# Two empty turns between the first one-hot blocks and their products in an attention and routing kernel

## The chip, the cores and the metric

The kernel runs on one core of one Trainium2 chip. The metric is the device time in microseconds (us) of one execution. The engines are TensorE (PE: matrix products and transposes into PSUM), VectorE (DVE), ScalarE (ACT), GpSimd (POOL) and SyncE (SP, which issues most of the DMA transfers). Each engine works through its own queue in order; semaphores tie the queues together.

## The reference

```python
q_pool = q.reshape(B, H, S // 2, 2, D).mean(axis=3)          # B 4, H 8, S 1152, D 64
scores = softmax(q_pool @ k.T / sqrt(D)) ; attn = scores @ v  # 4 x 8 x 576 x 64
x = attn -> [2304 tokens, 512]
do_compute = x @ w_skip > 0                                   # tokens that go to an expert
e_idx = argmax(x @ w_gate) ; gate_w = its softmax probability # 8 experts
y = gate_w * relu(x @ w1[e_idx]) @ w2[e_idx] ; x = x + y      # for the tokens that compute
out = ((x @ m1) * (x @ m2)) @ w3 @ w_out                      # second block, all tokens
```

## The kernel before, in words

The 4 images of the batch have 8 heads each; two heads make a pair, so there are 16 pairs p, four to an image. A pair is worked in 9 tiles of 128 pooled queries. The loop (L772) runs over turns i; p and l are the quotient and remainder of i by 9. A turn is a software pipeline over tiles. In the order in which TensorE gets its work, turn i does this:

- 9 transposes (L305) of the softmax numerators of tile i - 2. ACT, VectorE and ACT evacuate the three banks (L324). After the second evacuation the loop calls `side("D")`, which gives one step to other work, described below.
- ACT's exponential of tile i - 1 (L294).
- 8 products with v (L341), which accumulate in one of two fixed banks, VB[0] or VB[1].
- 6 score products of tile i (L271; 9 with three operand pairs in the fifth tile of a pair), and VectorE's row maximum (L282).
- In turns with l in 8, 0, 1, 3, 4, 5, if a routing step of kind "P" is due, that step with the accumulation bank that is free (L828).
- Preparation of the pairs to come: POOL splits keys and queries into a high and a low part (`prep`, L224 to L238), and SP copies them to the operand tiles.

Two generators run beside this. `conv_ops` converts the weights of the last block from 64-bit numbers to 32-bit ones, in 40 chunks: POOL squares (L96), VectorE takes bits apart (L111 to L119), SP loads and stores. `route_ops(b)` routes image b: it begins at i = 44, 80 and 116 for images 0 to 2, and after the loop for image 3. It yields "P" ahead of a step for TensorE and "D" ahead of a small step for VectorE. `side(kinds)` advances the routing if the step due is of one of these kinds; otherwise the conversion.

Routing an image takes these steps: normalisers and gate products (two "P" steps), transposes of the logits (two), argmax and one-hot of the expert (five "D"), prefix sums (one "P", L408), index arithmetic (two "D"; the second ends with the cast into `hf_`, L434). Then POOL builds one-hot blocks, one for each 128 tokens, five in all, in a ring of two buffers `ob` (L441 and L444, four instructions each): two at once, each further one after the product of the block whose buffer it takes. A block's product on TensorE (two instructions, L465) writes token numbers to their slots, which VectorE adds to `slots` (L467). After the fifth come the gate sums (one "D", L479) and five "P" steps that transpose the attention output to rows (L487), scale them on VectorE (L490, L493) and store them (L495).

In image 3 the routing has a hook: VectorE builds all five blocks at once, and the products are at L456. After the loop follow the product of the two last weight matrices, the expert tiles and the last block.

Of the kernel before, what the change touches and what calls it, by code (L numbers as in the profile page):

```python
# [17 lines left out]
NE, D, F = 8, 512, 1024  # L18
# [26 lines left out]
def body(ctx, tc, q, k, v, w9, w1, w2, m1, m2, w3t, wo, cst, mcst, ids, out, dbg=None):  # L45
# [89 lines left out]
    if True:  # L135
# [13 lines left out]
        def tbank():  # L149
            return free["b"]  # L150
# [4 lines left out]
        def load(p):  # L155
            if p >= NP:
                return
            b, hp = divmod(p, NHP)
            rawq[p] = erl.tile([128, 2, SQ], F32, tag="qr", name="qr", bufs=2)
            rawk[p] = erl.tile([128, S], F32, tag="kr", name="kr", bufs=1)  # L160
            SP.dma_start(rawk[p], k[b, hp])
            SP.dma_start(rawq[p], q[b, hp])
# [23 lines left out]
        def load_v(p):  # L186
            if p >= NP:
                return
            b, hp = divmod(p, NHP)
            vr = mid.tile([128, 2, KT, HD], F32, tag="vr", name="vr", bufs=2)  # L190
            SP.dma_start(vr, v[b, 2 * hp:2 * hp + 2].rearrange("h (p t) d -> p h t d", p=128))
            rawv[p] = vr
# [21 lines left out]
        def ld_kh(h):  # L214
            SP.dma_start(f(KH[0][64 * h:64 * h + 64]), f(KS[0][h][0:64]))
# [137 lines left out]
        def route_ops(b, hook=None, obs=None):  # L353
# [84 lines left out]
            def build(j):  # L438
                t = ob[j] = obs[j % len(obs)]
                for u in range(2):  # L440
                    E.tensor_scalar(t[:, 128 * u:128 * u + 128], iota[:, 0:128], hf_[:, 0, u, j:j + 1], None,  # L441
                                    op0=ALU.is_equal)
                for u, c0, n in ((0, 256, NSL), (1, 256 + NSL, NCNT)):
                    E.tensor_scalar(t[:, c0:c0 + n], iota[:, 0:n], hf_[:, 1, u, j:j + 1], idf[:, b, j:j + 1],  # L444
                                    op0=ALU.is_equal, op1=ALU.mult)

            parts = ((0, 0, NSL), (1, NSL, NCNT))
            for j in range(len(obs)):
                build(j)
            if len(obs) == NTT:  # L450
                yield "P"
                tp = tbank()
                for u, c0, n in parts:
                    for j in range(NTT):
                        t = ob[j]
                        PE.matmul(tp[:, c0:c0 + n], lhsT=t[:, 128 * u:128 * u + 128], rhs=t[:, 256 + c0:256 + c0 + n],  # L456
                                  start=(j == 0), stop=(j == NTT - 1))
                DVE.tensor_tensor(slots, tp[:, 0:NSL + NCNT], slots, op=ALU.add)
            else:
                for j in range(NTT):  # L460
                    yield "P"
                    tp = tbank()
                    t = ob.pop(j)
                    for u, c0, n in parts:
                        PE.matmul(tp[:, c0:c0 + n], lhsT=t[:, 128 * u:128 * u + 128], rhs=t[:, 256 + c0:256 + c0 + n],  # L465
                                  start=True, stop=True)
                    DVE.tensor_tensor(slots, tp[:, 0:NSL + NCNT], slots, op=ALU.add)  # L467
                    if j + len(obs) < NTT:
                        build(j + len(obs))
# [30 lines left out]
        def side(kinds):  # L500
            k = rts.get("k")
            if k and k in kinds:
                rts["k"] = next(rts["g"], None)
            elif k != "D":
                next(conv, None)

        def emit_meta(scratch):
# [56 lines left out]
        def wprime_fill():  # L564
            wp = tctx.enter_context(tc.tile_pool(name="wp", bufs=1, side="right", reuse_waits="tile"))
            CC = [wp.tile([128, 8, D], F32R, name=f"CC{x}") for x in "hl"]
            RW = [wp.tile([128, 8, 128], F32, name=f"RW{i}") for i in range(3)]
            WS = [[wp.tile([128, 8, 128], F32R, name=f"WS{x}{i}") for x in "hl"] for i in range(3)]
            wv.update(CC=CC, RW=RW, WS=WS)
            wov = wd["wo"].rearrange("(a p f) -> p a f", p=128, f=D)  # L570

            def ld_rw(u):
                SP.dma_start(RW[u % 3], wd["w3t"].rearrange("(u p a f) -> u p a f", u=8, p=128, f=128)[u])
            wv["ld"] = ld_rw
            for u in range(2):
                ld_rw(u)
                SP.dma_start(f(CC[1][:, 4 * u:4 * u + 4]), wov[:, 4 * u:4 * u + 4])
            ld_rw(2)
            yield
            for u in range(3):  # L580
                POOL.tensor_scalar(WS[u][0], RW[u], 1.0, 0.0, op0=ALU.mult, op1=ALU.add)
                POOL.tensor_tensor(WS[u][1], RW[u], f(WS[u][0]), op=ALU.subtract)
                ld_rw(u + 3)
                yield
            for a in range(8):
                POOL.tensor_scalar(CC[0][:, a], f(CC[1][:, a]), 1.0, 0.0, op0=ALU.mult, op1=ALU.add)
                POOL.tensor_tensor(CC[1][:, a], f(CC[1][:, a]), f(CC[0][:, a]), op=ALU.subtract)
                if a % 2:
                    yield
# [158 lines left out]
        with tc.manual_schedule():  # L748
# [23 lines left out]
            for i in range(NSTEP + 7):  # L772
                p, l = divmod(i, NT9)
                if i == NSTEP - NT9 + 1:
                    for _ in conv:
                        pass
                    ectx.close()
                    wfill = wprime_fill()
                if i > NSTEP - NT9:
                    next(wfill, None)  # L780
                if l == (4 if p == 0 else 1):
                    load(p + 2)
                if l == 7 and p >= 1:
                    load_v(p + 1)
                it = i - 2
                tr = 0 <= it < NSTEP
                ss = i < NSTEP
                pvs = []
                for n in (2 * i - 13, 2 * i - 12):
                    pp, r = divmod(n, 18)  # L790
                    pvs.append((pp, *divmod(r, 9)) if 0 <= pp < NP else None)
                if (i - 36 - 8) >= 0 and (i - 36 - 8) % 36 == 0 and (i - 44) // 36 < NB - 1:
                    rts["g"] = route_ops((i - 44) // 36)
                    rts["k"] = next(rts["g"])
                if tr or ss:
                    st_s[i] = ps_s.tile([128, 3, 512], F32, tag="s", name="s")
                evac = []
                if tr:
                    for g in range(3):
                        emit_t(it, g, i, evac)  # L800
                        emit_c(it, g, EV[g], evac)
                        if g == 1 and i > 5:
                            side("D")
                if 1 <= i <= NSTEP:
                    emit_e(i - 1)
                for u in pvs:
                    if u:
                        emit_pv(*u)
                if ss:
                    for g in range(3):  # L810
                        emit_s(i, g, evac)
                    emit_x(i)
                    if i == 0:
                        prep_q(1, DVE, 0, 256, sq[1])
                        for c in range(3):
                            prep_k(1, 384 * c, 384 * c + 384)
                        ld_kh(1)
                        for h in range(2):
                            prep_q(h, POOL, 256, SQ, sr[h])
                        next(conv)  # L820
                        DVE.tensor_copy(base, cs[:, C_EOFF:C_EOFF + NC_])
                        DVE.tensor_copy(csr, cs[:, C_U:C_U + 256])
                    if i == 2:
                        PE.matmul(VB[1][:, 0:128], lhsT=ones, rhs=tri, start=True, stop=True)
                        DVE.tensor_copy(iota[:, 0:128], VB[1][:, 0:128])
                        DVE.tensor_scalar(iota[:, 128:NSL], iota[:, 0:NSL - 128], 128.0, None, op0=ALU.add)
                        DVE.tensor_scalar(idf, idt, 1.0, None, op0=ALU.add)
                if l in (8, 0, 1, 3, 4, 5) and rts.get("k") == "P":  # L828
                    free["b"] = VB[1] if l in (8, 0, 1) else VB[0]
                    side("P")  # L830
                if ss and p == 0 and l < 3:
                    prep(1, l)
                if i == 4:
                    next(conv)
                if ss and l >= 6:
                    prep(p + 2, l - 6)
                if ss and l in ((3, 4) if p == 0 else (4, 5)):
                    prep(p + 1, l if p == 0 else l - 1)
# [207 lines left out]
```

## Time and profile before

| | us |
|---|---|
| median of 3 runs | 1090.47 (1088.94 to 1090.56) |
| the profiled execution | 1092.66 |
| its span, first to last instruction | 1090.8 |
| TensorE busy in the span | 1038.4 (95%) |
| VectorE, ACT, POOL busy | 598.0, 482.4, 387.0 |
| the attention loop | about the first 558 us |

Rows of the timeline give the start, the duration, the engine, the line, the operation with output and inputs, and in brackets how long the engine had been idle before it and what released it. One row can merge neighbouring instructions of one line (x9); its duration is then from the first's start to the last's end. Ends of products are modelled and overlap the next product's start, so the pace of TensorE is read from start to start. A granted clock of 1.00 is 2.4 GHz, 0.50 is 1.2 GHz.

### The profile page before, as it was taken

The numbers are of one execution on the slowest core, as the hardware profiler recorded it, in microseconds if no ns is written. First come the engines' busy times: TensorE is split into PE (matmuls) and PEld (weight loads), VectorE is DVE, ScalarE is ACT, GpSimd is POOL, SyncE is SP. The second block draws the span as 40 slices with busy tenths as digits, with TensorE's granted clock in tenths as the row PEclk, the third lists the DMA queues.
The fourth block names the chain that finished last, engine by engine and source line by source line (L and its number), as shares of the span: only waits on it lengthen the run. The fifth ranks groups of instructions, "written<-read, shape, count | busy, mean of one in ns | idle before, by whom it ended". The sixth has DMA issues, their size and how long they took to land. (4 is left out here: it accounts for less than half of the span.)

```text
span 1090.8 us, 16927 instructions
## 1 busy us (share of the span) xinstructions
PE 1038.4 (95%) x6101; PEld 839.9 (77%) x6101; DVE 598.0 (55%) x934; ACT 482.4 (44%) x902; POOL 387.0 (35%) x426
## 2 busy tenths in 40 slices
PE   6999999999999999999999999998799999999996
PEld 5677776677766777667667778786799998989895
DVE  5888887688986888755637422437531221212120
ACT  4666666565665666555532322334432221212121
POOL 4754433672536724351620523439201010101101
PEclk9999999999999999989998999999899999999999
DMA  9887778377973678714702761507101010101000
GB/s 256 259 239 192 216 218 232 101 182 212 268 224 98 185 214 256 183 40 101 238 20 74 247 225 40 190 25 243 34 11 50 10 49 20 39 20 39 29 2 30
DMA packets 68237, 144.83 MB, mean 133 GB/s; under 512 B 12960, under 2 KB 22560, under 8 KB 68130
## 3 DMA queue, kind: packets, MB, share of 16 engines
q1 hardware_dynamic: 63330, 129.28, 41.1%
q0 software_dynamic: 4800, 14.24, 4.0%
q8 instruction: 53, 0.87, 0.3%
q14 instruction: 54, 0.44, 0.1%
HBM read 86.21 MB, written 22.87 MB: 100 GB/s over the span
## 5 line engine op out<-in xcount | busy, mean ns | idle before, releaser
L282 DVE TENSOR_REDUCE sm<-s 128x1 f32<-128x1152 f32 x144 | 195.2, 1356 | 108.4 <-PE s L271 88.3
L324 ACT COPY pt<-s 128x384 f32<-128x384 f32 x288 | 138.0, 479 | 184.4 <-PE s L305 184.1
L271 PE MATMUL s<-k,q 128*128 128x384 f32 x864 | 204.3, 364 | 15.5 <-DVE k L197 7.8
L271 PEld LDWEIGHTS s<-k,q 128*128 128x128 f32 x864 | 147.2, 193 | 83.8 <-issue 41.7
L294 ACT ACTIVATE p<-s,sm 128x1152 f32<-128x1152 f32 x144 | 176.3, 1225 | 10.0 <-DVE sm L282 9.7
L341 PE MATMUL vb<-pt,vr 128*64 128x256 f32 (+1 forms) x1152 | 173.9, 422 | 4.5 <-DVE xr L490 2.1
L305 PE MATMUL s<-cs,p 128*128 128x128 f32 x1296 | 172.0, 279 | 2.9 <-ACT p L294 2.9
L305 PEld LDWEIGHTS s<-cs,p 128*128 128x128 f32 x1296 | 151.5, 144 | 12.1 <-ACT p L294 6.2
L956 DVE TENSOR_TENSOR ar<-b,ar 128x384 f32<-128x384 f32 x48 | 26.8, 558 | 191.9 <-PE b L952 191.9
L341 PEld LDWEIGHTS vb<-pt,vr 128*64 128x64 f32 x1152 | 70.7, 137 | 59.4 <-issue 23.7
L971 POOL DMA_INDIRECT out_dram<-ar,slots x18 | 18.1, 1003 | 272.1 <-ACT ar L970 267.4
L324 DVE COPY pt<-s 128x384 f32<-128x384 f32 x144 | 78.9, 548 | 5.1 <-PE s L305 5.0
L225 POOL TENSOR_TENSOR kl<-kr,kh 128x384 fp32r<-128x384 f32 x45 | 47.6, 1058 | 73.0 <-DMA k<-kl 70.2
L957 ACT CAST CVh<-ar 128x384 fp32r<-128x384 f32 x48 | 24.6, 513 | 108.8 <-DVE ar L956 108.8
L96 POOL TENSOR_TENSOR cm<-ch 128x512 f32<-128x512 f32 x40 | 43.0, 1079 | 66.6 <-DVE ca L119 46.1
L560 PE MATMUL b<-W1h,CVh 128*128 128x512 f32 x176 | 60.5, 403 | 1.2 <-ACT CVh L691 0.7
L560 PE MATMUL b<-W2h,CVh 128*128 128x512 f32 x176 | 60.7, 405 | 0.3
L560 PE MATMUL b<-WPh,CVh 128*128 128x512 f32 x144 | 57.3, 398 | 0.0
L560 PE MATMUL b<-WPh,CVl 128*128 128x512 f32 x144 | 56.9, 395 | 0.0
L560 PE MATMUL b<-WPl,CVh 128*128 128x512 f32 x144 | 56.8, 395 | 0.0
L970 ACT COPY ar<-b 128x512 f32<-128x512 f32 x18 | 10.6, 586 | 86.2 <-PE b L560 86.2
L224 POOL TENSOR_SCALAR kh<-kr 128x384 fp32r<-128x384 f32 x45 | 27.2, 604 | 57.2 <-PE s L271 53.6
(210 smaller groups left out, 1816.7 us busy)
## 6 DMA issues: line engine op xcount, KB each, us to landing
R<-in_w_dram SPq DMA_DIRECT2D x16, 1024.0 KB, 7.1
vr<-in_v_dram SPq DMA_DIRECT2D x16, 576.0 KB
kr<-in_k_dram SPq DMA_DIRECT2D x15, 576.0 KB, 6.2
qr<-in_q_dram SPq DMA_DIRECT2D x15, 576.0 KB, 6.6
k<-kh SPq DMA_DIRECT2D x30, 288.0 KB, 5.6
k<-kl SPq DMA_DIRECT2D x30, 288.0 KB, 6.4
q<-qnl SPq DMA_DIRECT2D x60, 144.0 KB, 3.4
ch<-in_w3t_dram SPq DMA_DIRECT2D x16, 512.0 KB, 5.6
```

The costliest lines, as they stand in the source:

```text
L96: POOL.tensor_tensor(m, hf, hf, op=ALU.mult)
L224: POOL.tensor_scalar(KH[i][:, cc], rawk[p][:, cc], 1.0, 0.0, op0=ALU.mult, op1=ALU.add)
L225: POOL.tensor_tensor(KL[:, cc], rawk[p][:, cc], f(KH[i][:, cc]), op=ALU.subtract)
L271: m = PE.matmul(sp[:, c, 0:384], lhsT=lt, rhs=kk[:, 384 * c:384 * c + 384], start=(n == 0), stop=(n == len(seq) - 1))
L282: DVE.tensor_reduce(sm, sp[:, :, 0:384], axis=AX.XY, op=ALU.max, negate=True)
L294: ACT.activation(pt, sp[:, :, 0:384], AF.Exp, bias=sm, scale=1.0, accum_out=SM[b][:, hp, c:c + 1])
L305: m = PE.transpose(tp[:, u * 128:u * 128 + 128], src[:, kt * 128:kt * 128 + 128], ident)
L324: m = (DVE.tensor_copy(o, i_) if eng is DVE else ACT.copy(o, i_)).ins
L341: PE.matmul(acc[64 * h:64 * h + 64, 0:n], lhsT=vr[:, h, kt, :], rhs=pt[:, kt, h, :], start=(kt == 0), stop=(kt == KT - 1))
L560: PE.matmul(o, lhsT=lh[a], rhs=rh[b_], start=(first and n == 0), stop=(last and n == len(order) - 1))
L956: DVE.tensor_tensor(cv, pb[:, 0:GT], av, op=ALU.mult)
L957: ACT.copy(CV[0][:, c], cv)
```

## The change

After POOL has been given the first two blocks, the routing yields "C" twice, except for the image with a hook. The loop's call becomes `side("DC")`, so that a "C" step is passed there, one a turn. In such a turn the conversion advances as well, as it does in a turn in which no "D" step is due.

```diff
             for j in range(len(obs)):
                 build(j)
+            if not hook:
+                yield "C"
+                yield "C"
             if len(obs) == NTT:
                 yield "P"
...
             if k and k in kinds:
                 rts["k"] = next(rts["g"], None)
-            elif k != "D":
+            if kinds != "P" and k != "D":
                 next(conv, None)
...
                         if g == 1 and i > 5:
-                            side("D")
+                            side("DC")
```

## Rows read from the trace of the kernel before

**Rows 1.** The page: granted clock in 40 slices (tenths), and the costliest group.

```profile
PEclk9999999999999999989998999999899999999999
...
L282 DVE TENSOR_REDUCE sm<-s 128x1 f32<-128x1152 f32 x144 | 195.2, 1356 | 108.4 <-PE s L271 88.3
```

**Rows 2.** Waits of TensorE, whole span: total us, times, longest us.

```profile
PE s L271 <- DVE pt L324: 7.5, 11, 1.2
PE vb L465 <- POOL ob L444: 5.9, 3, 2.0
```

**Rows 3.** Timeline of TensorE, image 0, turns 55 to 59.

```profile
207.96 1.34 PE L271 MATMUL s<-k,q 128*128 128x384 f32 x6
211.29 0.75 PE L465 MATMUL vb<-ob 128*128 128x146 f32 x2 [1.99 <-POOL ob L444]
211.90 2.18 PE L305 MATMUL s<-cs,p 128*128 128x128 f32 x9
...
215.60 1.34 PE L271 MATMUL s<-k,q 128*128 128x384 f32 x6
216.78 1.14 PE L305 MATMUL s<-cs,p 128*128 128x128 f32 x9
...
220.04 0.28 PE L465 MATMUL vb<-ob 128*128 128x146 f32 x2
220.18 1.20 PE L305 MATMUL s<-cs,p 128*128 128x128 f32 x9
...
227.44 0.28 PE L465 MATMUL vb<-ob 128*128 128x146 f32 x2
```

**Rows 4.** Timeline of TensorE, image 1, turns 91 to 93.

```profile
344.54 1.34 PE L271 MATMUL s<-k,q 128*128 128x384 f32 x6
...
353.31 1.15 PE L305 MATMUL s<-cs,p 128*128 128x128 f32 x9
...
356.56 0.28 PE L465 MATMUL vb<-ob 128*128 128x146 f32 x2
```

**Rows 5.** Timeline of TensorE, image 2, turns 127 to 129.

```profile
481.65 1.34 PE L271 MATMUL s<-k,q 128*128 128x384 f32 x6
484.96 0.80 PE L465 MATMUL vb<-ob 128*128 128x146 f32 x2 [1.97 <-POOL ob L444]
...
491.71 1.15 PE L305 MATMUL s<-cs,p 128*128 128x128 f32 x9
```

**Rows 6.** Windows: length, busy us (instructions) by engine, granted clock, DMA share, GB/s.

```profile
211.80:215.20 3.40, 3.40 (x16) 2.65 (x18) 1.50 (x3) 1.56 (x3) 3.40 (x6) 0.50 0.00 0
215.30:348.00 132.70, 128.02 (x883) 95.69 (x879) 109.50 (x162) 82.22 (x157) 62.47 (x74) 1.00 0.72 200
...
484.90:491.60 6.70, 6.64 (x25) 5.04 (x26) 1.48 (x3) 2.17 (x4) 5.77 (x10) 0.50 0.37 93
```

**Rows 7.** Timeline of POOL, image 0, turns 55 to 62.

```profile
209.17 1.21 POOL L441 TENSOR_SCALAR ob<-iota,hf 128x128 fp32r<-128x128 f32 x2 [7.51 <-DVE hf L434]
...
214.06 1.63 POOL L441 TENSOR_SCALAR ob<-iota,hf 128x128 fp32r<-128x128 f32 x2
...
216.93 1.04 POOL L96 TENSOR_TENSOR cm<-ch 128x512 f32<-128x512 f32 x1
...
241.58 0.54 POOL L238 TENSOR_SCALAR bd<-qnl 64x64 fp32r<-64x64 f32 x2
```

**Rows 8.** Timeline of VectorE, turns 68, 71 and 138.

```profile
262.89 0.67 DVE L490 TENSOR_TENSOR xr<-vb,r 64x512 f32<-64x512 f32 x1
263.49 0.15 DVE L493 COPY xr<-ga 64x4 f32<-64x4 f32 x1
...
272.70 1.36 DVE L282 TENSOR_REDUCE sm<-s 128x1 f32<-128x1152 f32 x1
...
530.46 1.41 DVE L493 COPY xr<-ga 128x4 f32<-128x4 f32 x1
```

**Rows 9.** Waits of POOL, 0 to 560 us.

```profile
POOL kh L224 <- PE s L271: 53.6, 8, 17.3
```

## The prediction

> **What bounds the kernel now.** I read the page first. VectorE idles most before its maximum (L282), 108.4 us, of which score products of TensorE end 88.3 [rows 1]; so in the attention loop TensorE sets the pace, and idle time on it is time lost. Its granted clock is 9 tenths or more in every slice of the loop but the one from 464 us, which has an 8 [rows 1]: a first hint, and a coarse one, since a slice is 27 us long and hides a stretch of three. The list of TensorE's waits by line comes next [rows 2]. One group there has a single cause: the products of the one-hot blocks (L465) wait 5.9 us in three waits, 2.0 us at most, for POOL's L444.
>
> Then I opened TensorE's timeline around each of the three [rows 3 to 5]. In image 0, POOL starts the four one-hot instructions of block 0 at 209.17 us and is through block 1 at 214.06 [rows 7]; TensorE has finished its score products at about 209.3 and has block 0's product next in its queue. It starts that at 211.29 after 1.99 us of idling. What follows runs slowly: nine transposes take 2.18 us, where nine of the next turn take 1.14 [rows 3]. The windows say why: the granted clock is 0.50 (1.2 GHz) from 211.8 to 215.2, and 1.00 (2.4 GHz) from 215.3 to 348.0, up to the next of the three waits; the third is followed by 6.7 us at half clock [rows 6]. So each wait is paid twice: as idle time, and as slow work afterwards.
>
> **The change, step by step.** Number the turns of the loop by i; l is i mod 9. Image 0's routing starts at i = 44. At i = 55 (l = 1) its last index arithmetic runs and POOL gets blocks 0 and 1; in the same turn the product slot (l is in the list 8, 0, 1, 3, 4, 5) takes product 0. Now two "C" steps come between: i = 56 and 57 pass them, and the slot at the end of i = 57 (l = 3) takes product 0; products 1 and 2 go to 58 and 59, 3 and 4 to 62 and 63 (before: 55, 57, 58, 59, 62). The gate sums move from 63 to 64, the five blocks of transposed rows from 63, 64, 66, 67, 68 to 64, 66, 67, 68, 71. The weight conversion still advances in "C" turns, so it skips turn 64 instead of 63 and is otherwise unmoved. The same holds 36 and 72 turns later. The fourth image, after the loop, passes a hook and gets no empty turns. No instruction is added or removed.
>
> *What goes.* Image 0: from the start of the score products before the late product (207.96) to the transposes two turns on (216.78) are 8.82 us. Undisturbed, the same work is one set of score products, 215.60 to 216.78 = 1.18, and a turn without product, 216.78 to 220.04 = 3.26 [rows 3]. The product itself is still paid, later: 220.04 to 220.18 = 0.14, and 0.06 on the transposes behind it (1.20 against 1.14), together 0.20. Saved: 8.82 - 1.18 - 3.26 - 0.20 = 4.18. Image 1: 344.54 to 353.31 = 8.77; less 1.18, less 353.31 to 356.56 = 3.25, less 0.20: 4.14 [rows 4]. Image 2: 481.65 to 491.71 = 10.06; less 1.18, 3.25 and 0.20: 5.43 [rows 5]. Sum 13.8 us. Of image 0's 4.18, the part up to the transposes at 211.90 is 3.94 - 1.38 = 2.56 (waiting, with the second half of the product also late); 1.62 is slow clock.
>
> *What is late next.* Without the stall turn 56 ends at about 209.1 + 3.3 = 212.4 and turn 57 at 215.7. POOL is through block 1 at 214.06 as before, since its start hangs on VectorE's casts in turn 55; products 0 and 1 find their operands. Block 2 reuses block 0's buffer and starts after product 0, behind one square of the conversion (L96, 1.04 us [rows 7]) that the empty turns put ahead of it and that fits into POOL's idle time between 214.1 and 215.9. It needs 216.93 - 214.06 = 2.87 us at most and so is done by 219; product 2 comes two turns after product 0, 220.04 to 227.44 being 7.4 us [rows 3], at about 223. Cover: over 4 us. Block 3 has three turns, block 4 four.
>
> *What the moved pieces may cost.* Block 4 and the key and query splits behind it on POOL slide by up to 3 us against TensorE. Image 0's splits end at 242.12 [rows 7], and their copies to the operand tiles are issued in turn 67, near 256: 14 us of cover, cost nothing. Those copies go by SP's queue, in which the stores of transposed rows stand ahead of them as before. The last transposed block goes to turn 71 (l = 8), where POOL splits queries and VectorE has no idle time: its maximum at 272.70 begins without having waited for the score products [rows 8]. There 0.67 + 0.15 us are added (the 64-row forms of L490 and L493). How VectorE takes that no row shows; the nearest are a small copy of the same line that took 1.41 us instead of 0.15 while POOL worked [rows 8], and the longest wait of score products for VectorE's copy, 1.2 us [rows 2]. Ends: 0 and 1.2 per image; I take 0.4, nearer to the turns 66 to 68, which carry the same load and mostly show no wait, and for image 2 nothing, since turn 143 is the last with score products and the tail waits for ACT anyway. Together 0.8, ends 0 to 2.4. A gain there I exclude: work is only made later.
>
> The Trainium skill's page "SBUF — State Buffer", section "Who interferes with whom", says that VectorE and POOL share a pair of ports and that the second of two contending instructions waits for the whole of the first. The 1.41 us copy agrees [rows 8]. If every such copy in the moved blocks were held so, 1.26 us for each of two images, the sum would be 13.8 - 2.5 = 11.3.
>
> Net: 13.8 - 0.8 = 13.0. The profiled execution took 1092.66 us (span 1090.8 and 1.9 around it); with the change it would take 1079.7. The median of the timed runs is 1090.47, 2.2 less; the same 13.0 gives **1077.5 us**. Whether the timed runs have the long slow stretch of image 2 in the same place isn't shown: three images like image 0 would give 12.5, three like image 2 16.3, so 11.7 to 15.5 net of 0.8.
>
> **Rivals.**
> *A, the clock falls anyway.* If the half clock after 211.8 belonged to that place (its load, another engine) and not to the wait, only the waiting would be saved: 3 x 2.56 = 7.7, and 1082.8 us. For it: nothing but that the cause is inferred. Against: the slow stretches start within 0.6 us of a late product [rows 3, 5, 6], and the 132.7 us up to the next one are at full clock with the same work [rows 6]. The Trainium skill's page "TensorE: Matmul & The Clock Gate", section "HAM oscillation — how this bites in real kernels", warns of idle gaps longer than these, which speaks for A; the trace shows the fall after gaps of 2 us. Chance 0.07.
>
> *B, the wait moves to product 2.* If the square ahead of block 2 on POOL waited (for its load, or for a buffer), block 2 would be late and TensorE would idle at turn 59. It begins to cost from 4 us of delay and has taken the gain when the delay is 6.5 us (2.5 of waiting, then the slow clock). Only images 0 and 1 still convert; image 2's 5.4 stay: about 1085 us. Against: in the shown stretch the square ran without idling before it [rows 7]. Chance 0.05.
>
> *C, slower.* POOL's builds now end one product later, and the key and query splits of the pair after next queue behind them. If these reached the operand tiles late, the first score products of that pair would wait, and the slow clock would follow: 1.62 us and the wait. It decides from 14 us of delay on POOL, and loses more than the gain from about 17 (three more of waiting); at 18 us, 1 us per image is lost, 1093 us. Against: POOL idles 53.6 us before L224 waiting for TensorE's score products [rows 9], so it is ahead, not behind. Chance 0.03.
>
> *D, nothing moves.* If the two steps were swallowed (the slot rule would let product 0 in at turn 56 if l = 2 were in its list, which it isn't), 1090.5. Chance 0.02.
>
> **How the numbers follow.** Forecast 0.83, A 0.07, B 0.05, C 0.03, D 0.02. The forecast's own range is 1074.5 (gain 15.5 with a little beside it) to 1080 (11.3, less the spread of the runs, which cover 1.6 us). Stretched to A's edge: 1074.0 to 1082.0, which leaves out B to D, most of A and some of the forecast's own ends. 0.2% is 2.2 us, about what a measurement of this kernel tells from no change: faster by more than that, 0.94 (forecast, A, most of B); within it 0.03 (D, the rest of B); slower 0.03 (C).
>
> **What would show it.** In the profile after: no wait of L465 for POOL's L444 in the list of waits; product 0 some 6.5 us after POOL's first one-hot instruction, without idle before it; the granted clock 1.00 throughout from 30 us to the end of the loop; the three stretches 4.2, 4.1 and 5.4 us shorter; at turns 71 and 107 a wait of score products for L324 of some tenths. The forecast is wrong if a slow stretch stays where no wait precedes it (A), if L465 waits again at its third product (B), or if L271 waits for the splits of the keys (C).

## The result, and the profile after

The changed kernel takes 1076.76 us (median of 4 runs, 1076.03 to 1080.15) against 1089.93 us before: 13.2 us less, ratio 0.9886 with a 95% interval of 0.9863 to 0.9909. In two later comparisons the ratio was 0.9909 (0.9885 to 0.9933) and 0.9916 (0.9890 to 0.9942); by the medians of the three, 13.2, 11.9 and 9.0 us are gained. The profiled execution has a span of 1074.2 us against 1090.8.

TensorE's longest waits after, whole span (total us, times, longest us). The one-hot products are L468 now, three lines lower, and stand nowhere in the whole list, of which these are the first lines; before, L465 waited 5.9 us [rows 2]. The wait of score products for L324 is as it was (7.5 before).

```profile
PE s L271 <- DVE k L197: 7.7, 2, 6.5
PE s L271 <- DVE pt L324: 7.2, 10, 1.4
PE b L955 <- DVE W1l L916: 5.4, 1, 5.4
PE s L305 <- ACT p L294: 2.8, 3, 2.1
PE b L692 <- DMA xr<-x_d,ix: 2.6, 1, 2.6
```

TensorE's timeline after, image 0, turns 55 to 59, as in [rows 3]; the rows left out are the products with v and with other operands.

```profile
206.86 1.34 PE L271 MATMUL s<-k,q 128*128 128x384 f32 x6
208.04 1.15 PE L305 MATMUL s<-cs,p 128*128 128x128 f32 x9
...
210.13 1.34 PE L271 MATMUL s<-k,q 128*128 128x384 f32 x6
211.31 1.14 PE L305 MATMUL s<-cs,p 128*128 128x128 f32 x9
...
213.40 1.33 PE L271 MATMUL s<-k,q 128*128 128x384 f32 x6
214.57 0.28 PE L468 MATMUL vb<-ob 128*128 128x146 f32 x2
214.71 1.20 PE L305 MATMUL s<-cs,p 128*128 128x128 f32 x9
...
221.97 0.28 PE L468 MATMUL vb<-ob 128*128 128x146 f32 x2
```

The transposes of turn 56 follow the score products of turn 55 at once and take 1.15 us, not 2.18. From 206.86 to 211.31 are 4.45 us, before 8.82. Images 1 and 2 have the same stretch:

```profile
340.48 1.34 PE L271 MATMUL s<-k,q 128*128 128x384 f32 x6
...
344.92 1.14 PE L305 MATMUL s<-cs,p 128*128 128x128 f32 x9
...
472.99 1.34 PE L271 MATMUL s<-k,q 128*128 128x384 f32 x6
...
477.43 1.14 PE L305 MATMUL s<-cs,p 128*128 128x128 f32 x9
```

Both 4.44, before 8.77 and 10.06 [rows 4, 5]. With 0.20 for each product, paid later, the three stretches give 4.17, 4.13 and 5.42 us. The window of the loop (length, busy us and instructions of PE, PEld, DVE, ACT, POOL, granted clock, DMA share, GB/s) shows no half clock any more [rows 6]:

```profile
25.00:560.00 535.00, 523.87 (x3565) 388.18 (x3564) 414.97 (x612) 332.46 (x628) 259.58 (x298) 1.00 0.67 189
```

POOL's timeline after, image 0, beside [rows 7]:

```profile
208.06 1.20 POOL L441 TENSOR_SCALAR ob<-iota,hf 128x128 fp32r<-128x128 f32 x2 [7.84 <-DVE hf L434]
...
212.18 1.28 POOL L444 TENSOR_SCALAR ob<-iota,hf,idf 128x146 fp32r<-128x146 f32 x2
213.42 1.48 POOL L96 TENSOR_TENSOR cm<-ch 128x512 f32<-128x512 f32 x1
214.91 1.18 POOL L441 TENSOR_SCALAR ob<-iota,hf 128x128 fp32r<-128x128 f32 x2
216.07 1.98 POOL L444 TENSOR_SCALAR ob<-iota,hf,idf 128x146 fp32r<-128x146 f32 x2
```

Blocks 0 and 1 are ready at 213.46, the square of the conversion runs in the gap, block 2 is ready at 218.05, and its product starts at 221.97: 3.9 us of cover.

The 16.6 us between the two spans are: 13.7 in the three stretches; 1.1 ahead of turn 55 (206.86 against 207.96), which the change doesn't touch; 0.5 lost at turn 72; and 2.3 over the rest, where waits and clock differ from one execution to the next. So one pair of profiles doesn't measure the change to better than some 3 us. Measured by a part that is steadier, from the transposes of turn 44 to those of turn 145 on TensorE's timeline, three profiles of before give 388.7, 386.9 and 386.4 us and three of the changed kernel 374.8, 374.2 and 374.2: 13.0 us less. That measure ("the loop") is used below; "before" is then the mean of its three profiles, 387.3 us, and the changed kernel's mean is 374.4.

### The profile page after: what moved, and what is told of

The parts are those of the page before. It is cut to its first block, busy times and chain, and to the rows that moved or that the text cites. A ratio compares the mean times of both kernels' runs of the same rounds, so it can differ in the third digit from the quotient of the medians.

```text
span 1074.2 us, 16931 instructions
## 1 busy us (share of the span) xinstructions
PE 1027.9 (96%) x6101; PEld 833.2 (78%) x6101; DVE 594.7 (55%) x934; ACT 481.8 (45%) x902; POOL 387.0 (36%) x426
## 5 line engine op out<-in xcount | busy, mean ns | idle before, releaser
L271 PE MATMUL s<-k,q 128*128 128x384 f32 x864 | 203.1, 362 | 15.1 <-DVE k L197 7.7
L324 ACT COPY pt<-s 128x384 f32<-128x384 f32 x288 | 137.8, 479 | 168.5 <-PE s L305 168.2
L271 PEld LDWEIGHTS s<-k,q 128*128 128x128 f32 x864 | 146.0, 191 | 83.2 <-issue 40.8
L305 PE MATMUL s<-cs,p 128*128 128x128 f32 x1296 | 168.1, 275 | 2.8 <-ACT p L294 2.8
L305 PEld LDWEIGHTS s<-cs,p 128*128 128x128 f32 x1296 | 147.5, 142 | 12.7 <-ACT p L294 6.9
L324 DVE COPY pt<-s 128x384 f32<-128x384 f32 x144 | 78.7, 547 | 1.6 <-PE s L305 1.5
L96 POOL TENSOR_TENSOR cm<-ch 128x512 f32<-128x512 f32 x40 | 43.1, 1082 | 63.2 <-DVE ca L119 48.8
```

The costliest lines, as they stand in the source:

```text
L96: POOL.tensor_tensor(m, hf, hf, op=ALU.mult)
L271: m = PE.matmul(sp[:, c, 0:384], lhsT=lt, rhs=kk[:, 384 * c:384 * c + 384], start=(n == 0), stop=(n == len(seq) - 1))
L305: m = PE.transpose(tp[:, u * 128:u * 128 + 128], src[:, kt * 128:kt * 128 + 128], ident)
L324: m = (DVE.tensor_copy(o, i_) if eng is DVE else ACT.copy(o, i_)).ins
```

## The experiments

**Filler while POOL builds.** Is the half clock the wait's doing, or the place's?

```diff
                     t = ob.pop(j)
+                    if j == 0:
+                        for _ in range(15):
+                            PE.matmul(tp[:, 0:256], lhsT=ones, rhs=csr, start=True, stop=True)
                     for u, c0, n in parts:
```

> The kernel before, with 15 products of 128x256 put ahead of product 0 of images 0 to 2 (their result is overwritten by product 0): TensorE works while POOL builds, but the late product stays where it is. My theory (idling lets the clock fall, and the slow clock costs 1.6, 1.6 and 2.9 us): the granted clock stays 1.00 there, the 2 us of waiting stay as filler, so about 6 us less than before: 1084, ratio 0.9945. Rival A (the half clock belongs to that place, whatever TensorE did before): clock 0.50 as before, 1090, ratio 1.000 or slightly over.

TensorE's timeline, image 0, and two windows of it:

```profile
207.84 1.34 PE L271 MATMUL s<-k,q 128*128 128x384 f32 x6
209.01 1.95 PE L466 MATMUL vb<-csr 128*128 128x256 f32 x15
211.15 0.70 PE L468 MATMUL vb<-ob 128*128 128x146 f32 x2 [0.19 <-POOL ob L444]
211.70 1.20 PE L305 MATMUL s<-cs,p 128*128 128x128 f32 x9
...
215.01 1.14 PE L305 MATMUL s<-cs,p 128*128 128x128 f32 x9
```

```profile
208.50:216.00 7.50, 7.22 (x53) 6.05 (x51) 3.89 (x8) 3.02 (x8) 6.96 (x11) 1.00 0.01 3
...
23.00:570.00 547.00, 535.32 (x3636) 397.85 (x3634) 420.13 (x629) 334.19 (x632) 260.06 (x301) 1.00 0.67 187
```

Product 0 starts as late as before, yet the transposes behind it take 1.20 us instead of 2.18: the clock stayed at 1.00 here, with TensorE kept busy while POOL builds. 207.84 to 215.01 are 7.17 us: 1.65 less than before, 2.52 more than 4.45 + 0.20. The other images have the same stretch in 7.16 and 7.15. Rival A is out. The loop takes 380.8 us, 6.5 less than before, as expected. The timed runs do not show it: 1086.58 us, 1.9 less than the median before, ratio 0.9989 (0.9973 to 1.0004), which doesn't exclude no gain at all.

> The kernel before with the filler once more, for one look. Its first profile had the clock at 1.00 behind all three waits and 6 us less in the loop, but 3 to 5 us more after the loop, 4.9 of them in a wait of the first expert tile's transposes for gathered rows. If the filled kernel as such loses there, the wait is again over 4 us; if it is an accident of that execution, it is 0 to 3 us as in the other profiles, and the time is near 1082 to 1084. The clock is expected at 1.00 behind all three waits again; one fall there would speak against idling as its cause.

The clock again stayed at 1.00 and the loop took 381.5 us. The wait for gathered rows (L692) was 2.4 us, not over 4. The time was 1088.02, not the 1082 to 1084 expected, beside a single run of the kernel before of 1086.41. TensorE's two longest waits behind the loop:

```profile
PE b L955 <- ACT W2h L915: 6.8, 1, 6.8
...
PE b L692 <- DMA xr<-x_d,ix: 2.4, 1, 2.4
```

From turn 145 to the last product the filled kernel took 533.5 and 532.1 us in its two profiles, before 530.0 to 530.6, the changed kernel 528.6 to 531.0. So 1.5 to 3.5 of the 6 us are given back after the loop. The two waits together are 9.2 us here and 11.3 in the first filled profile, against 4.7 to 6.0 before; but they are 8.0 in the changed kernel's first profile, whose part after the loop is shorter than before (528.6), so they don't explain it alone. Why the filled kernel takes longer after the loop stays open. For the timed gain one number on record helps: each timed run lists TensorE's granted clock over its whole span. Its mean is 0.9883 for the 12 runs of the filled kernel and 0.9859 for the 23 before. If TensorE sets the pace throughout, the share missing from full speed is time lost, and the difference of 0.0024 is worth 2.6 us of 1088 (an estimate from these numbers). So the timed runs of the two kernels differ less in slow clock than the loops of their profiles, which differ by 6 us. Where the timed runs lost their clock is not recorded.

**The change for image 0 alone.**

```diff
-            if not hook:
+            if b == 0:
                 yield "C"
                 yield "C"
```

> The change for image 0 alone. My theory (each image pays 4.2 us, image 2 in the profile 5.4): about 4 us less than before, 1086, ratio 0.9964; the profile has two waits of the one-hot products for POOL, in images 1 and 2, each with the half clock behind it, and a full clock around the products of image 0. Rival (a gain that comes from somewhere else, once for all images, such as the conversion's turns): either nothing or the most part of 13 us.

1086.25 us, 2.2 less than the median before where about 4 were expected, ratio 0.9987 (0.9970 to 1.0003), so the timed runs alone don't show it; the loop takes 382.5 us, 4.9 less than before. The two waits left are there, but look at what follows each, image 1 first:

```profile
344.42 0.69 PE L468 MATMUL vb<-ob 128*128 128x146 f32 x2 [1.96 <-POOL ob L444]
344.96 1.20 PE L305 MATMUL s<-cs,p 128*128 128x128 f32 x9
...
479.31 0.69 PE L468 MATMUL vb<-ob 128*128 128x146 f32 x2 [1.96 <-POOL ob L444]
479.86 2.17 PE L305 MATMUL s<-cs,p 128*128 128x128 f32 x9
```

The same wait, 1.96 us, is followed by full clock in image 1 and by half clock in image 2. In image 1 the granted clock is 1.00 from 344 to 349 us, beyond these transposes too, and the stretch of two turns lost only 2.5 us. A fall after each wait, as expected, is refuted: half clock can follow the wait but doesn't have to.

**The kernel before, profiled twice more.**

> A second look at the kernel before. Theory of the first profile: all three waits are followed by half clock in every execution (loss 4.2, 4.1, 5.4 us). Rival, from the run with the change for image 0 alone, whose wait in image 1 left the clock at 1.00: the clock falls after some of the waits only, so the three losses lie between 2.5 and 5.4 us and differ from execution to execution.

> A third look at the kernel before, with the same two theories: half clock after each of the three waits, or only after some.

The second execution had half clock after all three waits, the third after those of images 0 and 2 only; its image 1:

```profile
346.04 0.69 PE L465 MATMUL vb<-ob 128*128 128x146 f32 x2 [1.97 <-POOL ob L444]
346.59 1.20 PE L305 MATMUL s<-cs,p 128*128 128x128 f32 x9
```

In image 0 of the third execution the clock fell later than elsewhere, behind the transposes: they still take 1.20 us, and it is the products with v and the score products that are slow (1.08 and 1.31 to 1.34 us at full clock).

```profile
210.61 1.20 PE L305 MATMUL s<-cs,p 128*128 128x128 f32 x9
211.74 1.97 PE L341 MATMUL vb<-pt,vr 128*64 128x256 f32 x8
213.65 1.99 PE L271 MATMUL s<-k,q 128*128 128x384 f32 x6
```

So one group behind a wait doesn't tell; the whole stretch does. Over the three profiles of the kernel before and the one with the change for image 0 alone, the clock fell after 9 of 11 waits; with the filler in place of the idling it fell after none of 6. By the stretches from turn 55 to 57, the loss per image was 4.0 to 4.2 us in most cases, 5.4 where the slow clock lasted 6.8 us, and 2.5 where the clock stayed; its sum was 13.7 in the first profile, 12.3 and 12.0 in the others. What decides whether the clock falls is not shown.

**Distance without empty turns.** Only the list of turns for routing products is changed in the kernel before:

```diff
-                if l in (8, 0, 1, 3, 4, 5) and rts.get("k") == "P":
+                if l in (8, 0, 3, 4, 5) and rts.get("k") == "P":
```

> The kernel before without any empty turn, but with l = 1 taken from the list of turns that take a step of kind P. Product 0 can then not fall into the turn in which POOL gets its blocks; it goes to turn 57 as in the changed kernel. My theory (only the distance between building and product counts): the wait for POOL and the half clock vanish as with the empty turns, 13 us; beyond that the waits of the products with v for VectorE's L380 and L490 in the turn behind a slot at l = 1 (1.9 and 2.1 us in three waits each) go too, so 16 to 17 us less than before, 1073, ratio 0.985. Rival (those waits only move to the next slot): 1077, ratio 0.988, as the changed kernel. Rival (the empty turns do something of their own): near 1090.

> The kernel before without the slot at l = 1, once more beside the changed kernel on one chip. Theory: 4 us less than the changed kernel, since the waits for L380 and L490 in the turns with l = 2 are gone in the loop (4.0 us in six waits) and nothing else differs that costs: 1073 against 1077. Rival (the 2.8 us seen first were spread of the runs): within 1 us of it.

1073.79 us, ratio 0.9884 (0.9858 to 0.9910), beside 1076.55 for the changed kernel; again 1072.63, ratio 0.9865 (0.9837 to 0.9893), beside 1079.06. The loop takes 370.4 and 370.1 us, 4.2 less than with the empty turns.

The edit moves the builds as well. The routing's earlier products also skip l = 1, so the last index arithmetic comes a turn later, in turn 56, and product 0 at turn 57 is one turn behind its build, not two. Image 1, where it is tightest, on POOL's and on TensorE's timeline:

```profile
344.03 1.83 POOL L444 TENSOR_SCALAR ob<-iota,hf,idf 128x146 fp32r<-128x146 f32 x2
```

```profile
345.88 0.32 PE L465 MATMUL vb<-ob 128*128 128x146 f32 x2
```

Block 0 is ready at 345.86, 0.02 us before its product starts; in images 0 and 2 the cover is 0.3 and 0.6 us. In the changed kernel it is about 3 to 3.5 us. So one turn of distance was just enough here. TensorE's waits from 0 to 560 us, with product 0 at turn 57:

```profile
PE s L271 <- DVE k L197: 7.7, 2, 6.6
PE s L271 <- DVE pt L324: 6.7, 11, 1.3
PE s L305 <- ACT p L294: 2.1, 2, 1.7
PE vb L456 <- DVE R L444: 0.9, 2, 0.5
PE vb L341 <- ACT pt L324: 0.3, 2, 0.2
```

The waits for POOL are gone without a "C", and so are those of the products with v for L380 and L490, which the changed kernel keeps (L490 is L493 there):

```profile
PE vb L341 <- DVE xr L493: 2.1, 3, 0.7
...
PE vb L341 <- DVE lw L380: 1.9, 3, 0.6
```

Together they are 4.0 us, about what the loop gains beyond the changed kernel. By the medians this version is 2.8 and 6.4 us faster than the changed kernel, and it beats the kernel before clearly.

**The changed kernel again**, beside the others:

> The changed kernel once more, beside the others on one chip. My theory: 13 us less than before (ratio 0.988), no wait of the one-hot products for POOL and no half clock in the loop after its start. The rival (noise or another cause made the first comparison): a ratio nearer to 1.

> The changed kernel beside it: 1077, 12 to 13 us less than before, ratio 0.988 to 0.990, no wait of the one-hot products, the clock at 1.00 from 25 us to the end of the loop for the third time.

1076.55 and 1079.06 us, ratios as given at the top: 11.9 and 9.0 us less than before, the first a little and the second clearly under the 12 to 13 expected. Neither profile has a wait of L468 for POOL, and the clock was 1.00 from 25 us to the end of the loop in both.

**Three empty turns.** One more `yield "C"`.

> The changed kernel with three empty turns: product 0 goes to turn 58 (l = 4), the five products to 58, 59, 62, 63, 64, the transposed rows to 66, 67, 68, 71, 72. My theory (the wait is gone with the first free slot, more distance buys nothing; each block of rows moved to l = 8 or 0 costs some tenths): as the changed kernel to 1 us more, 1077, ratio to before 0.990; no wait of the one-hot products. Rival (the blocks came just in time with two, and more distance gains further): 1 to 2 us less than the changed kernel.

1078.25 us, ratio 0.9894 (0.9869 to 0.9920); the loop takes 374.7 us, as with two. More distance buys nothing: product 4 falls to l = 1 and brings a wait that the row blocks used to bring there.

```profile
PE vb L341 <- DVE slots L471: 2.4, 3, 1.2
```

In the other direction: with one "C" instead of two the program is the same, instruction for instruction on every engine, because turn 56 (l = 2) has no slot anyway. The second "C" adds nothing: either way product 0 comes two turns behind its build.

**Filler in the changed kernel**, 15 products in turn 55, ahead of the first "C":

```diff
             if not hook:
+                lp = tbank()
+                for _ in range(15):
+                    PE.matmul(lp[:, 0:256], lhsT=ones, rhs=csr, start=True, stop=True)
                 yield "C"
```

> The changed kernel with the 15 products of 128x256 issued in turn 55 of images 0 to 2, as pure extra work of TensorE (their result is used by nobody): 1.95 us each by the profile of the kernel before with the same filler. My theory (TensorE sets the pace of the loop, so its time is the kernel's time): 3 x 1.95 = 5.9 us more than the changed kernel, 1082.5, ratio to before 0.995. Rival (2 us of TensorE there are partly absorbed by a later wait): less, 1077 to 1080. Rival (a later start of what comes after the loop costs more than the delay, as the 1086.6 us of the filled kernel before would have it): 1084 to 1086.

1083.61 us, ratio 0.9942 (0.9920 to 0.9964), 4.5 to 7 us more than the changed kernel's medians in the other comparisons, 5.4 more than the kernel with three empty turns in the same one. That is near the 5.9 expected, but by the timed runs alone the second rival, 1084 to 1086, isn't excluded. In its image 0 the filler takes from 205.22 to 207.09, 1.87 us; the loop takes 378.7 us, 4.3 more than 374.4. So three quarters of the extra work are paid in the loop: TensorE sets the pace there, though small waits take up some of it: from 23 us to the end of the loop score products wait 4.5 us for L324, and 5.1 to 5.8 in the changed kernel's three profiles.

## Why the prediction was right

The result lies where it was forecast, 1077.5 against 1076.8, by the steps that were forecast. That it came within 1 us is in part luck, as the second point below shows.

*What goes.* 4.18, 4.14 and 5.43 us per image were worked out; the profile shows 4.17, 4.13 and 5.42. The split held as well: 2.56 of image 0 was called waiting and the rest slow clock. The filler, which takes away the idling and leaves the delay, kept 2.52, and the images whose clock did not fall lost 2.5.

*The size of the sum* is right for the first profile and a little too large in general. The half clock was taken to follow every wait; the range allowed for the length of a slow stretch, not for its absence. With 9 falls of 11 and the three profiles' sums, 12.0 to 13.7, the stretches are worth 12.7 us on the mean. Less the 0.5 paid for the moved pieces, that is 12.2. The first timed gain, 13.2 us, lies above it; the later ones, 11.9 and 9.0 by the medians, lie below, and the interval of the last ends at 12.0 us. The granted clocks of the timed runs point the same way: in these two comparisons the mean is 0.9859 and 0.9853 before, 0.9892 and 0.9883 changed. By the estimate used for the filler, the difference is worth 3.6 and 3.3 us, while the means of the profiles, 0.984 and 0.991, would make it 7. So the profiled executions of the kernel before seem to have lost more to the slow clock than most timed ones, and the sum was read from such a profile.

*What is late next.* Nothing in the way forecast against: product 2's cover was put at over 4 us and measured 3.9, so B stays out; L271 does not wait for the splits of keys, so C stays out; the square did go into POOL's gap.

*What the moved pieces cost* was put at 0.4 us each for images 0 and 1, through a VectorE copy held by POOL behind turn 71. It is 0.53 in image 0 and nothing in image 1. VectorE's, POOL's and TensorE's timelines after:

```profile
268.56 0.67 DVE L493 TENSOR_TENSOR xr<-vb,r 64x512 f32<-64x512 f32 x1
269.16 1.23 DVE L496 COPY xr<-ga 64x4 f32<-64x4 f32 x1
270.31 0.54 DVE L324 COPY pt<-s 128x384 f32<-128x384 f32 x1
```

```profile
268.95 1.41 POOL L230 TENSOR_TENSOR qsum<-qr 128x576 f32<-128x576 f32 x1
```

```profile
270.90 0.97 PE L271 MATMUL s<-k,q 128*128 128x384 f32 x4 [0.53 <-DVE pt L324]
```

The copy of four columns takes 1.23 us, where it took 0.15 before [rows 8]: it ends as POOL's addition, which began earlier, does. The score products then wait for the copy behind it. In image 1 POOL's addition ended at 402.30 us, before the copy began at 402.81; the copy took 0.26 us and no score products wait for the one behind it. That is what the Trainium skill's page "SBUF — State Buffer", section "Who interferes with whom", says of the two engines' shared ports; this row and the one of before agree.

*Rival A* is refuted by the filler: same place, same delay, full clock. The page of the Trainium skill "TensorE: Matmul & The Clock Gate", which in its section "HAM oscillation — how this bites in real kernels" warns of longer idle gaps only, differs from the rows: half clock came after 9 of 11 idle gaps of 2 us here.

*The profiled time* was put at 1079.7 and came out at 1076.0. Of these 3.7 us, 1.1 lie ahead of turn 55 and 2.3 over the rest, which the change doesn't touch, and 0.3 in the moved pieces.

## What to carry to other kernels

A queue that reaches a product before its operand is built pays once for the wait and may pay again for the slow clock after it; look at what the instructions behind a wait cost, not only at the wait. Where a generator deals out work in slots, count in slots how far the consumer lies behind its producer; here a build in the turn before the product was just enough (0.02 to 0.6 us of cover), and leaving out the slot that caused the collision (l = 1) also removed two other waits, which the empty turns left in place. Measure a change of 1% in the stretch that it touches, over several profiles, before reading anything into a few us of the whole span.

## What was not expected

Waits of 1.96 to 1.99 us were followed by half clock in 9 cases and by full clock in 2, and the slow stretch lasted 3.4 us or 6.8. And 6 us saved in the loop by the filler came to only 2 in the timed runs, with 1.5 to 3.5 us more after the loop, whose waits differ by several us between kernels that are equal there.
